# Word conversion of the first eight weight tiles and the first group's division in a fused attention, FFN and expert kernel

## The chip, the cores and the metric

One core of a Trainium2 chip runs the whole program. The metric is device time in microseconds (us) of one execution; the time before is the median of three runs.

## The reference, cut to what matters

Three stages follow one another over 4 x 576 = 2304 tokens of 512 channels (8 heads of 64).

```python
# 1 attention with random features, per batch and head
phi(x): proj = x @ omega.T; h = proj - |x|^2/2; exp(h - max(h)) / sqrt(m)      # m = 128
kv = k_p.T @ v ; z = sum(k_p) ; out = (q_p @ kv) / (q_p @ z + 1e-6)
# 2 feed-forward, w_in and w_out are float64
h = x @ w_in ; g = h * clip(h + 3, 0, 6) / 6 ; x = g @ w_out                    # 512 -> 2048 -> 512
# 3 top-1 of 8 experts
e = argmax(x @ w_gate + modality_bias[modality_id]) ; out = gate * (relu(x @ w1[e]) @ w2[e])
```

The weights `w_in` and `w_out` arrive as float64, so each value is two 32-bit words, and the kernel makes the float32 value of them on the chip.

## The kernel before, in words

The 2304 tokens are nine groups of 256 (`NG`), of two tiles of 128 rows (`GT`). The 8 heads are four pairs (`NPR`); a unit is one pair with one batch (for k) or with one group (for q).

*How the order is set.* No order is written out. Every piece of work is a generator that hands its next instruction to a list scheduler (`Issue.run`, line 255), which keeps a modelled clock for each engine (`cost`, line 79), takes the engine whose next instruction could start first, and among the instructions that could start within 0.08 us of that one the one with the lowest priority number. The program's instruction order on each engine is fixed by this when the program is built; on the chip each engine runs its list in order. Priorities: the first group's units -1.0 (`FIRST`), the feed-forward activations -0.8, the word conversions -0.3 (`CONVERT`), the weight splits -0.25, the loads -0.1, the products 0.05. An operation that may run on several engines is given to the one that the model says ends first.

*The first group.* `early(pr)`, line 1327, runs for each of the four pairs a k unit of batch 0 (`k_unit`) and then the q unit of group 0 (`q_unit`, line 804). Buffers for these come from the ring `w`, so the trace calls them all `w`. A q unit projects with TensorE, takes the maximum on VectorE (`mx`), takes four exponentials on ScalarE (`phi`, line 571), forms four sums with `z` on VectorE (`junk`, with the sum in `den`), adds a constant, takes the reciprocal, multiplies each of its four 128 x 128 blocks by its column of `den` (line 849, one instruction per block, on VectorE, ScalarE or GpSimd), transposes with TensorE (`ident`), copies to SBUF on ScalarE (`k.qe`), multiplies by `kv` on TensorE, and is copied as `x`. For group 0 the PSUM banks are kv/kp, y0/y1, qa/qb and h0/h1 for the four pairs.

*The words.* There are 32 tiles of float64 weights, tile j holding 128 x 512 word pairs: even j is a tile of `w_in`, odd j of `w_out` (`loads`, line 472). The first eight (`NW0`) land in the ring `w`, the others in four buffers `words`. `convert` (line 509) turns a tile into float32: ScalarE makes the three low bits from the upper 16 bits of the low words (an int32 out of uint16 values, line 519), VectorE ORs the sign in from the high word (line 523), ScalarE multiplies the high words by 2^-112 in place (line 526), and VectorE shifts them left by 3 and ORs them in (line 527). Three workers (`NC`) take tiles in turn, j, j+3, and so on; tiles from 8 on wait until the four first units are over.

*The feed-forward.* Step c of group 0 needs x of all four pairs and tile 2c (`t_in`, products into `h`), then `r` by ScalarE and VectorE, then tile 2c+1 (`t_out`, products into `y`). Group 0 multiplies the float32 tiles as they are; the groups after it use tiles split in two (`split_w`, line 543). While group 0's sixteen steps run, the k units of batches 1 to 3 (`kp`, `kv`) and the q units of group 1 (`qa`, `qb`) run between them.

Of the kernel before, what the change touches and what calls it, by code (L numbers as in the profile page):

```python
# [12 lines left out]
I32 = mybir.dt.int32  # L13
AF = mybir.ActivationFunctionType
ALU = mybir.AluOpType
# [19 lines left out]
def f32(ap):  # L35
    return ap.bitcast(F32)
# [9 lines left out]
class Issue:  # L46
# [178 lines left out]
    def op(self, e, m, cond=None, **kw):  # L225

        es = [e] if isinstance(e, str) else list(e)
        outs, ins = self.aps(kw)
        g = Gate([(x, ins, outs, self.cost(x, m, kw)) for x in es], cond)
        yield g  # L230
        x = es[g.pick]
        if x == "A" and m == "tensor_copy":
            kw = dict(out=kw["out"], in_=kw["in_"], func=AF.Copy)
            m = "activation"
        if x == "A" and m == "tensor_scalar":
            kw = dict(out=kw["out"], in_=kw["in0"], func=AF.Copy, scale=kw["scalar1"])
            m = "activation"
        self.do(x, m, **kw)
# [63 lines left out]
def favor_ffn_top1_moe_kernel(  # L302
# [37 lines left out]
    NW0 = 8  # L340
# [9 lines left out]
    do, op = q.do, q.op  # L350
# [47 lines left out]
    def split(hi, lo, src, hi_eng=("A", "V"), lo_eng="V"):  # L398
        yield from op(hi_eng, "tensor_copy", out=hi, in_=src)
        yield from op(lo_eng, "tensor_tensor", out=lo, in0=src, in1=f32(hi), op=ALU.subtract)  # L400

    def tt(o, a, b, f, e="V"):
        return op(e, "tensor_tensor", out=o, in0=a, in1=b, op=f)

    def ts(o, a, s1, f1, s2=None, f2=None, e="V"):
        kw = dict(out=o, in0=a, scalar1=s1, scalar2=s2, op0=f1)
        if f2 is not None:
            kw["op1"] = f2
        return op(e, "tensor_scalar", **kw)
# [54 lines left out]
    w_in_t, w_out_t, w_full = {}, {}, {}  # L464
# [3 lines left out]
    def conv():  # L468

        staged, whole, parts, done, cut, short, issued = {}, {}, {}, set(), set(), [], set()  # L470

        def loads():
            for j in range(NW):
                c = j // 2
                yield Gate(cond=lambda: st["early_k"] == n_streams and (j < NW0 + NB or j - NB in done))
                w = q.tile(*((wp, [P, DM, 2], I32, "w", NW) if j < NW0 else (const, [P, DM, 2], I32, "words", NB)))
                issued.add(j)
                if j % 2 == 0:
                    src = w_in[:, c * P:(c + 1) * P, :].rearrange("(k p) f w -> p k f w", p=P)
                    yield from op("S", "dma_start", out=w.rearrange("p (k f) w -> p k f w", k=KD), in_=src)  # L480
                else:
                    yield from op("S", "dma_start", out=w, in_=w_out[c * P:(c + 1) * P])
                staged[j] = w

            for j in range(NB):
                yield Gate(cond=lambda: NW - NB + j in done)
                w = q.tile(const, [P, E // NB, DM], F32, "words", NB)
                for e in range(E // NB):
                    yield from op("S", "dma_start", out=w[:, e], in_=w_gate[len(wg):len(wg) + 1, :].to_broadcast([P, DM]))
                    wg.append(w[:, e])  # L490

        def place(c, which):

            if c < WC:
                yield Gate(cond=lambda: c in whole)
                return whole[c][:, which, :]
            if len(short) >= 4 and short[-4] not in cut:
                yield Gate(cond=lambda: short[-4] in cut)
            short.append(2 * c + which)
            return q.tile(ff, [P, DM], F32, "st", 4)  # L500

        def places():
            yield Gate(cond=lambda: NW0 - 1 in issued)
            for c in range(WC):
                if c == NW - NW0 - 3 * n_streams:
                    yield Gate(cond=lambda: st["early"] == n_streams)
                whole[c] = q.tile(wp, [P, 2, DM], F32, "w", NW)

        def convert(j):
            c, which = j // 2, j % 2  # L510
            yield Gate(cond=lambda: j in staged)
            t = yield from place(c, which)
            w = staged.pop(j)
            lo_w, hi_w = w[:, :, 0], w[:, :, 1]


            ti = t.bitcast(I32)
            half = w.rearrange("p n w -> p (n w)").bitcast(U16).rearrange("p (n w) -> p n w", w=4)
            yield from op(
                "A", "activation", out=ti, in_=half[:, :, 1], func=AF.Copy, scale=2.0 ** -13, bias=2.0 ** -14 - 0.5  # L520
            )

            yield from op(
                "V", "scalar_tensor_tensor", out=ti, in0=hi_w, scalar=-(1 << 31), in1=ti, op0=ALU.bitwise_and, op1=ALU.bitwise_or
            )
            yield from ts(f32(hi_w), f32(hi_w), 2.0 ** -112, ALU.mult, e="A")
            yield from op(
                "V", "scalar_tensor_tensor", out=ti, in0=hi_w, scalar=3, in1=ti,
                op0=ALU.logical_shift_left, op1=ALU.bitwise_or,
            )  # L530
            done.add(j)
            w_full[which, c] = t

        def gone(k):

            if k < 3 * n_streams:
                return st["early"] == n_streams
            c = k - 3 * n_streams - NW0
            if c < 0:
                return c + NW0 in done  # L540
            return 2 * c in cut and 2 * c + 1 in cut and min(st["n_in"], st["n_out"]) > c

        def split_w(j):

            c, which = j // 2, j % 2
            yield Gate(cond=lambda: len(whole) == WC and (which, c) in w_full and len(parts) == j
                       and gone(j - NW + WC + NW0 + 3 * n_streams) and (c < WC or st["n_out" if which else "n_in"] > c))
            t = parts[j] = q.tile(wp, [P, 2, DM], F32R, "w", NW)
            yield from split(t[:, 0], t[:, 1], w_full[which, c], ("A", "P"))
            cut.add(j)  # L550
            (w_out_t if which else w_in_t)[c] = t

        def splitter(k, n):
            for j in range(k, NW, n):
                yield from split_w(j)

        def worker(k, n):
            for j in range(k, NW, n):
                if j >= NB * 2:
                    yield Gate(cond=lambda: st["early"] == n_streams)  # L560
                yield from convert(j)

        q.add(loads(), LOADS)
        q.add(places())
        for k in range(NC):
            q.add(worker(k, NC), CONVERT)
        for k in range(2):
            q.add(splitter(k, 2), CUT)
# [230 lines left out]
    def q_units(k, units, tag):  # L799
        for g, pr in units:  # L800
            yield from q_load(k, g, pr)
            yield from q_unit(k, g, pr, [tag])

    def q_unit(k, g, pr, tags):
# [10 lines left out]
        else:  # L815
# [7 lines left out]
            for t in range(GT):  # L823
                c = slice(t * P, (t + 1) * P)
# [11 lines left out]
        for t in range(GT):  # L836
            for o, n, b, s in runs(g * G + t * P, P):
                for h in range(2):
# [3 lines left out]
                        in1=z_t[b, pr][o:o + n, h, :], op0=ALU.mult, op1=ALU.mult, accum_out=den[o:o + n, i:i + 1],  # L842
                    )
        yield from ts(den, den, 1e-6 * M, ALU.add)
        yield from op("V", "reciprocal", out=den, in_=den)
        if k.two:
            yield from tt(qp, qp, den.unsqueeze(2).to_broadcast([P, 2 * GT, M]), ALU.mult)
        else:
            for i in range(2 * GT):
                yield from ts(qp[:, i], qp[:, i], den[:, i:i + 1], ALU.mult, e=("V", "A", "P"))  # L850
# [6 lines left out]
        for o, n, b, s in rr:  # L857

            for h in range(2):
                c = slice(h * D, (h + 1) * D)  # L860
# [447 lines left out]
    with ExitStack() as ph, tc.manual_schedule():  # L1308
# [18 lines left out]
        def early(pr):  # L1327
            k = k_bufs_early()
            yield from k_unit(k, 0, pr, early_banks[pr])
            yield Gate(cond=lambda: k.loaded > len(k_parts))  # L1330
            yield from q_unit(k, 0, pr, early_banks[pr][:2])
            st["early"] += 1
            gone_by.add(pr)
# [138 lines left out]
```

## Time and profile before

| | |
|---|---|
| time before, median of 3 runs | 834.08 us (831.96 to 835.83) |
| profiled execution, its own time | 834.48 us |
| its span in the trace | 832.8 us |
| TensorE busy over the span | 791.0 us (95%) |
| VectorE busy | 630.8 us (76%) |
| ScalarE busy | 487.1 us (58%) |
| GpSimd busy | 99.7 us (12%) |
| mean granted TensorE clock | 0.983 |

Busy shares are over the whole span; the stages differ much, so the views by stretch say more than this table. PE is TensorE, DVE VectorE, ACT ScalarE, POOL GpSimd, SP SyncE. All of the kernel's instructions are issued from one helper, so that every row carries line 223; the tiles tell them apart. The modelled end of a matmul includes time in which it waited in the pipeline.

### The profile page before, as it was taken

How to read it: one execution, taken by the hardware profiler on the slowest of the kernel's cores; microseconds unless marked ns; L12 is line 12 of the kernel's file. 1: busy time of each engine (PE TensorE's matmuls, PEld its weight loads, DVE VectorE, ACT ScalarE, POOL GpSimd, SP SyncE). 2: the span in 40 equal slices, each digit the busy share in tenths (PEclk: the TensorE clock that was granted, in tenths of full speed). 3: DMA queues.
4: the chain of work that ended last, by engine and by line, in shares of the span. 5: the costliest groups of instructions: out<-in, count | busy, mean ns of one | idle time of the engine just before them, and what ended most of it. 6: DMA issues, size and time to landing. Idle time of an engine off the chain costs nothing.

```text
span 832.8 us, 16519 instructions
## 1 busy us (share of the span) xinstructions
PE 791.0 (95%) x5395; PEld 675.0 (81%) x5395; DVE 630.8 (76%) x2135; ACT 487.1 (58%) x1245; POOL 99.7 (12%) x114
## 2 busy tenths in 40 slices
PE   7799999999999999999999999998995999999994
PEld 5476668888888888888888888987884898999993
DVE  3889999888888868878788785667986777777610
ACT  3998786777757556555655453335445766555411
POOL 0132342000000000110000000002013122211000
PEclk9989999999999999999999999999997999999997
DMA  7717574222113022221120010009359899877300
GB/s 182 278 52 228 168 243 132 51 54 83 51 33 81 13 53 68 32 61 47 41 64 27 1 39 1 26 15 289 94 171 293 276 289 273 270 219 207 103 13 29
DMA packets 108767, 96.88 MB, mean 116 GB/s; under 512 B 14847, under 2 KB 90111, under 8 KB 108672
## 3 DMA queue, kind: packets, MB, share of 16 engines
q1 hardware_dynamic: 104976, 85.75, 35.8%
q0 software_dynamic: 3696, 9.98, 3.5%
q8 instruction: 45, 0.74, 0.4%
q14 instruction: 50, 0.41, 0.2%
HBM read 86.10 MB, written 9.87 MB: 115 GB/s over the span
## 4 chain that ended last, share of the span: by engine, by line
issue 36%; PE 33%; DMA 15%; DVE 8%; ACT 4%; POOL 1%; SPq 1%; POOLq 0%; DVEq 0%; ACTq 0%
PE h L223 14%; PE y L223 9%; DMA wraw<-in_w_dram 5%; DMA order<-og,pi 4%; DVE w L223 4%; PE qa L223 3%; PE qb L223 3%; ACT w L223 2%; PE kv L223 2%; PE kp L223 2%; DMA xr<-yrows,src 1%; DMA kraw<-in_kT_dram 1%; SPq L223 1%; POOL order L223 1%; DMA w<-in_v_dram 1%
## 5 line engine op out<-in xcount | busy, mean ns | idle before, releaser
L223 PE MATMUL h<-x,w 128*128 128x256 f32 x2616 | 367.6, 290 | 2.1 <-DVE gl L223 0.9
L223 PEld LDWEIGHTS h<-x,w 128*128 128x128 f32 x2616 | 343.0, 191 | 22.5 <-issue 3.8
L223 PE MATMUL y<-w,gh 128*128 128x512 f32 x640 | 205.2, 402 | 0.0
L223 PE MATMUL y<-w,gl 128*128 128x512 f32 x320 | 126.0, 394 | 0.0
L223 PEld LDWEIGHTS y<-w,gh 128*128 128x128 f32 x640 | 110.2, 190 | 18.2 <-issue 3.0
L223 DVE TENSOR_TENSOR w<-wraw,w 128x512 fp32r<-128x512 f32 x160 | 106.3, 687 | 20.3 <-ACT w L223 16.4
L223 ACT ACTIVATE w<-wraw 128x512 fp32r<-128x512 f32 x152 | 91.2, 627 | 29.1 <-DMA wraw<-in_w_dram 25.7
L223 ACT ACTIVATE r<-h,three 128x256 f32<-128x256 f32 x144 | 68.1, 473 | 62.5 <-PE h L223 52.4
L223 DVE SCALAR_TENSOR_TENSOR junk<-st,words 128x512 bf16<-128x512 f32 x144 | 98.8, 686 | 1.2
L223 ACT ACTIVATE gh<-r 128x256 fp32r<-128x256 f32 x126 | 52.5, 417 | 80.3 <-PE y L223 75.1
L223 DVE SCALAR_TENSOR_TENSOR r<-r,h 128x256 f32<-128x256 f32 x144 | 60.3, 419 | 28.2 <-ACT r L223 24.8
L223 DVE TENSOR_TENSOR gl<-r,gh 128x256 fp32r<-128x256 f32 x128 | 54.3, 424 | 34.4 <-ACT gh L223 22.0
L223 PEld LDWEIGHTS y<-w,gl 128*128 128x128 f32 x320 | 60.5, 189 | 14.3 <-DVE gl L223 0.3
L223 POOL DMA_INDIRECT order<-og,pi x18 | 19.1, 1064 | 406.9 <-DVE pi L223 261.4
L223 ACT ACTIVATE gh<-h 128x256 fp32r<-128x256 f32 x72 | 27.4, 380 | 60.1 <-PE qb L223 22.4
L223 DVE SCALAR_TENSOR_TENSOR gl<-h,gh 128x256 fp32r<-128x256 f32 x72 | 30.4, 422 | 31.9 <-ACT gh L223 29.1
L223 ACT ACTIVATE kp<-kp,mx 112x128 f32<-112x128 f32 (+1 forms) x120 | 38.8, 387 | 1.2 <-DVE mx L223 1.0
L223 POOL DMA_INDIRECT out_dram<-st,tok x19 | 19.8, 1040 | 162.5 <-ACT gh L223 77.7
L223 DVE SCALAR_TENSOR_TENSOR junk<-qp,zb 128x128 bf16<-128x128 f32 (+1 forms) x144 | 37.4, 286 | 1.4 <-ACT qp L223 0.2
L223 ACT ACTIVATE qp<-qp,mx 128x128 f32<-128x128 f32 x104 | 36.2, 393 | 0.0
L223 DVE SCALAR_TENSOR_TENSOR w<-words,w 128x512 int32<-128x512 int32 x44 | 31.7, 748 | 0.0
L223 PE MATMUL kp<-om,khl 128*112 128x256 f32 (+1 forms) x140 | 29.4, 307 | 1.5 <-DVE khl L223 1.0
(270 smaller groups left out, 1069.4 us busy)
## 6 DMA issues: line engine op xcount, KB each, us to landing
wraw<-in_w_dram SPq DMA_DIRECT2D x160, 256.0 KB
words<-in_w_in_dram SPq DMA_DIRECT2D x12, 512.0 KB
words<-in_w_out_dram SPq DMA_DIRECT2D x12, 512.0 KB
qraw<-in_qT_dram SPq DMA_DIRECT2D x36, 128.0 KB
yrows<-st SPq DMA_DIRECT2D x18, 256.0 KB
kraw<-in_kT_dram SPq DMA_DIRECT2D x40, 112.0 KB
vraw<-in_v_dram SPq DMA_DIRECT2D x24, 112.0 KB
w<-in_w_in_dram SPq DMA_DIRECT2D x4, 512.0 KB
```

What stands on the lines that cost most here:

```text
L223: return getattr(self.eng[e], m)(**kw)
```

## The change

Two edits. In `convert`, the tiles with j below 8 take another way: ScalarE multiplies the high words by 2^-112 in place first; VectorE multiplies the result by 2^-126 into the output tile, which leaves only the sign; VectorE shifts the low words right by 29 and ORs the three bits in; VectorE shifts the high words left by 3 and ORs them in. The tiles from 8 on are as before. In `q_unit`, the units of group 0 multiply their four blocks by `den` with one VectorE instruction, as units with `k.two` did already.

```diff
@@ convert(j), after lo_w, hi_w = w[:, :, 0], w[:, :, 1]
+            if j < NW0:
+
+                ti = t.bitcast(I32)
+                yield from ts(f32(hi_w), f32(hi_w), 2.0 ** -112, ALU.mult, e="A")
+                yield from ts(t, f32(hi_w), 2.0 ** -126, ALU.mult)
+                for w_, n, f in ((lo_w, 29, ALU.logical_shift_right), (hi_w, 3, ALU.logical_shift_left)):
+                    yield from op(
+                        "V", "scalar_tensor_tensor", out=ti, in0=w_, scalar=n, in1=ti, op0=f, op1=ALU.bitwise_or
+                    )
+                done.add(j)
+                w_full[which, c] = t
+                return
@@ q_unit(k, g, pr, tags)
-        if k.two:
+        if k.two or not g:
             yield from tt(qp, qp, den.unsqueeze(2).to_broadcast([P, 2 * GT, M]), ALU.mult)
         else:
             for i in range(2 * GT):
                 yield from ts(qp[:, i], qp[:, i], den[:, i:i + 1], ALU.mult, e=("V", "A", "P"))
```

## Rows read from the trace of the kernel before

**Rows 1.** Busy time of each engine by stretch (count), granted clock, DMA share, GB/s.
```profile
20.00:30.00 10.00, 8.21 (x105) 5.70 (x104) 6.46 (x14) 7.95 (x30) 0.00 (x0) 1.00 1.00 363
30.00:40.00 10.00, 5.65 (x36) 4.14 (x36) 9.38 (x49) 9.84 (x33) 1.15 (x2) 0.96 0.65 228
40.00:50.00 10.00, 10.00 (x54) 6.67 (x54) 6.95 (x15) 9.07 (x25) 5.00 (x8) 0.70 0.18 49
60.00:80.00 20.00, 19.90 (x128) 14.11 (x128) 19.39 (x44) 17.36 (x46) 6.56 (x6) 1.00 0.76 238
100.00:150.00 50.00, 48.64 (x305) 36.06 (x303) 48.30 (x111) 39.43 (x98) 16.98 (x14) 1.00 0.53 162
600.00:700.00 100.00, 89.39 (x569) 80.32 (x568) 77.61 (x179) 59.64 (x124) 23.90 (x22) 0.95 0.86 258
```
**Rows 2.** Chain of waits from 18 to 60 us: start, length, what.
```profile
32.58 0.99 ACT w L223 x4
...
35.55 1.52 ACT w L223 x6
...
37.12 2.64 ACT w L223 x6
...
39.80 1.12 PE kv L223 x4
40.92 1.35 PE y L223 x4
...
47.38 1.73 PE h L223 x8
```
**Rows 3.** ScalarE's groups by form, 28 to 46.7 us: busy, mean ns, idle before.
```profile
L223 ACT ACTIVATE w<-w 128x512 f32<-128x512 f32 x6 | 4.3, 776 | 0.0
L223 ACT ACTIVATE w<-w 128x128 f32<-128x128 f32 x10 | 3.3, 436 | 0.0
L223 ACT ACTIVATE w<-w 128x512 int32<-128x512 uint16 x4 | 2.7, 717 | 0.0
```
**Rows 4.** ScalarE in order of time: start, length, instruction, count.
```profile
38.01 0.69 ACT L223 ACTIVATE w<-w 128x512 int32<-128x512 uint16 x1
38.58 0.68 ACT L223 ACTIVATE w<-w 128x512 int32<-128x512 uint16 x1
41.88 0.72 ACT L223 ACTIVATE w<-w 128x128 f32<-128x128 f32 x2
42.17 0.43 ACT L223 ACTIVATE w<-w 128x128 f32<-128x128 f32 x1
```
**Rows 5.** VectorE in order of time, in brackets its idle time before.
```profile
27.53 0.42 DVE L223 TENSOR_REDUCE mx<-qb 128x2 f32<-128x256 f32 x1 [1.56 <-PE qb L223]
31.63 1.28 DVE L223 SCALAR_TENSOR_TENSOR w<-w 128x512 int32<-128x512 int32 x2
43.69 0.84 DVE L223 SCALAR_TENSOR_TENSOR w<-w 128x512 int32<-128x512 int32 x1 [0.81 <-ACT w L223]
46.20 0.69 DVE L223 SCALAR_TENSOR_TENSOR w<-w 128x512 int32<-128x512 int32 x1 [1.68 <-ACT w L223]
```
**Rows 6.** Groups by form of the whole run: busy, mean ns, idle before.
```profile
L223 DVE TENSOR_TENSOR qp<-qp,den 128x512 f32<-128x512 f32 x26 | 17.9, 687 | 0.2
L223 DVE SCALAR_TENSOR_TENSOR w<-w 128x512 int32<-128x512 int32 x16 | 11.1, 705 | 2.6 <-ACT w L223 2.5
L223 DVE CAST w<-wraw 128x512 fp32r<-128x512 f32 x8 | 3.4, 426 | 1.6 <-DMA wraw<-in_w_dram 1.6
```
**Rows 7.** The first group's blocks on GpSimd, 20 to 60 us, by form.
```profile
L223 POOL TENSOR_SCALAR w<-w 128x128 f32<-128x128 f32 x5 | 4.0, 806 | 36.1 <-DVE junk L223 36.1
```
**Rows 8.** TensorE by microsecond: stretch, busy, granted clock, DMA share, GB/s.
```profile
36.00:37.00 1.00, 0.00 (x0) 1.00 0.19 62
...
39.00:40.00 1.00, 0.20 (x2) 0.57 0.00 0
40.00:41.00 1.00, 1.00 (x5) 0.50 0.00 0
...
46.00:47.00 1.00, 1.00 (x11) 1.00 0.00 0
```

## The prediction

> **What bounds the kernel now.** I read the busy time by stretch first, then the chain of waits through the stretch that the change touches, then the engines' own order there, and last the groups by form for prices.
>
> The stretches [rows 1] show two regimes. From 60 us on TensorE is the bound: 19.90 of 20 us, 48.64 of 50. From 20 to 40 us it is not: 8.21 and 5.65 of 10, while ScalarE is busy for 7.95 and then 9.84, and VectorE for 6.46 and then 9.38. Everything that the diff touches lies in this start, before the first product of the feed-forward at 47.4 us. What the change can bring is therefore the time at which that first product starts; behind it TensorE has the same products to do, and I carry the shift to the end one for one.
>
> The chain of waits [rows 2] says what that start hangs on. Its rows from 32.58 through 39.76 us are ScalarE's, nearly without a break (16 exponentials, three divided blocks, word conversions, a copy): about 7.2 us in which the chain follows ScalarE. Then TensorE takes over at 39.80, and the chain stays on it until the first product. TensorE's own microseconds [rows 8] show why those take so long: it did nothing from 36 to 37, and from 39 to 46 us the granted clock is about 0.5, the lower of its two levels (1.2 GHz), with the engine busy all the time from 40 on. It rises again in the microsecond from 46.
>
> So there are three parts: ScalarE up to 39.8, TensorE at its lower level up to 46, TensorE at 2.4 GHz after it. VectorE is nearly as full as ScalarE from 30 to 40 us, and that is what decides this case.
>
> **The change part by part.** *Prices.* ScalarE's word instructions start 0.57 us apart (38.01, 38.58) and its divided blocks 0.29 apart (41.88, 42.17) [rows 4]. Of VectorE's word instructions two in a row take 1.28 us, so 0.6 us each from start to start, beside a duration of 0.705 [rows 5, 6]. The new division is an operation that later units already use: 128 x 512 by `den` takes 0.687 us [rows 6], again 0.6 from start to start.
>
> *The multiplication by 2^-126* has no row: 128 x 512 float32, one input that skips every other word. From below, the nearest is the cast of a dense 128 x 512 tile, 0.426; from above, the two-input word instruction on the same skipping input, 0.705 [rows 6]. It reads a single tensor in SBUF like the first and skips like the second. I take the middle, 0.55, and keep both ends: 3.4 to 5.6 us for eight of them. The Trainium skill, VectorE: DVE Perf Modes, section "What auto-detection actually checks", asks for a single source and a destination in SBUF with fitting outer dimensions for its two-results mode and names no dense step; by that rule the price is the lower end, and the eight cost 3.4 us instead of my 4.4. No row of this trace shows that mode on a skipping input.
>
> *What ScalarE loses.* One instruction of each of the eight tiles, 8 x 0.57 = 4.6 us, and ten divided blocks, 10 x 0.29 = 2.9 us [rows 3, 4]: 7.5 in all. From 28 to 46.7 us it had 6 + 4 word instructions [rows 3]; six tiles would now need six. Of the chain's 7.2 us on ScalarE, two conversions (1.14) and three blocks (0.88) go: 2.0 us, and one more conversion at most, 2.6. But a tile that follows sooner puts its own ScalarE instruction into the freed place, because the three workers no longer pass to and fro between the engines (before: ScalarE, VectorE, ScalarE, VectorE; now ScalarE once, then VectorE three times). I take half of 2.6: a gain of 1.3 us.
>
> *What VectorE gains.* Eight multiplications, 4.4, and four divisions of 0.6, 2.4, less a block that it did itself: about 6.6 us, where it stood still for 1.56, 0.81 and 1.68 us at the three largest breaks between 25 and 47 us [rows 5], 4.05 together. The words have slack: the first product needs tile 0, its second stage tile 1, and a step takes two tiles, so the later of the eight can be done after 47 us. What has no slack is the four sums of each unit before the reciprocal. The first unit's division (0.6) now stands ahead of other units' sums on VectorE: a loss of 0.6. The other three divisions follow their own sums and replace ScalarE's and GpSimd's blocks (five, 4.0 us of GpSimd [rows 7]), which were spread over three engines; TensorE at its lower level takes some 1 us for a unit's four transposes, longer than the 0.6 of a division, so these are hidden behind the unit before. If TensorE ran at 2.4 GHz that cover would be gone, at 0.1 us a unit or so.
>
> *What stays.* From 40.92 us TensorE itself sets the pace, and neither edit removes anything there. The conversions' order of loads and the queue of SyncE get nothing new; a buffer of tiles 0 to 7 comes free at most about 0.6 us later.
>
> *Sum.* -1.3 + 0.6 = -0.7 us at the first product. The profiled execution took 834.48 us, 1.7 more than its span of 832.8 and 0.4 more than the median; on the median the sum is 834.08 - 0.7 = 833.4 us. About 0.5% (4.2 us) is what a measurement of this kernel tells from no change.
>
> **The rivals.** *Faster: ScalarE was the whole bound.* The chain lies on ScalarE for 7.2 us, which speaks for it. Then all of the 2.6 us goes, and with TensorE resuming earlier its clock may not fall: the stretch from 40.9 to 46 at the lower level, 5.1 us, would take half, 2.6 less. Together 834.1 - 5.2 = 828.9 us. Against it: VectorE at 9.38 of 10 from 30 to 40 us [rows 1] has no room to follow, and the idle microsecond from 36 to 37 [rows 8] waits on the sums of VectorE as well.
>
> *Slower: VectorE becomes the bound of the start.* Place: the sums from 34 to 40 us. Each word instruction that VectorE begins just before a maximum or a sum is ready holds it for up to 0.6 us, and now up to three of a tile stand ready at once. If six of the eight multiplications at the upper price (0.6 from start to start, 3.6) and the first three divisions (1.8) lie ahead of the last sum, the first product comes 5.4 us later, less 0.6 that ScalarE gives: 838.9 us. It decides from the point at which more than 4.8 us of the added work lies ahead of that sum. Against it: the priority of the first units (-1.0 against -0.3) lets a word in only where nothing of theirs is ready.
>
> *Another order later.* The scheduler's modelled clocks move, so the order of all instructions behind may differ. From 600 to 700 us TensorE stands still for 10.6 us [rows 1], in the stage where transfers of expert weights arrive; such gaps can grow or shrink by a few us whatever the start does. Priced at 3 to 5 us of either sign: 829 or 838 us. Against it: the products and their transfers are the same, and in the stretches from 60 to 150 us little is idle that could change.
>
> *No effect at all*, because the freed ScalarE time and the added VectorE time cancel: 834.1, which is inside the forecast's own case.
>
> **How the numbers follow.** Forecast (0.58): the shift lies between -3 and +3 us, 831 to 837, likeliest 833.4. ScalarE the whole bound: 0.17. VectorE the bound: 0.10. Another order: 0.15, of which 0.08 faster by over 0.5%, 0.04 slower and 0.03 within. Faster 0.25, within 0.5% 0.61, slower 0.14. The range from 828 to 838.5 takes in the faster rival's value and nearly the slower one's; some 0.15 lies outside it.
>
> **What would show it.** In the profile of the changed kernel: ScalarE's busy time from 20 to 50 us falls by 4 to 7 us and VectorE's rises by about as much, with its breaks gone; the multiplication by 2^-126 takes between 0.43 and 0.70 us; the first product of the feed-forward starts at 46.7, give or take 2; TensorE's lower level appears around 39 to 46 us again. The forecast is wrong if the first product moves by over 4 us, if TensorE's clock holds through 40 to 46 us, or if the first product stands where I say and the end moves otherwise: then it was the order of the later stages.

## The result: 1.4% slower, and little of it in the start

| | before | after |
|---|---|---|
| median on the same chip | 834.96 us (831.96 to 836.29, 4 runs) | 846.10 us (839.29 to 850.46, 4 runs) |
| ratio, 95% interval | | 1.0137 (1.0102 to 1.0172) |
| profiled execution, its span | 834.48, 832.8 us | 842.66, 840.6 us |
| TensorE busy over the span | 791.0 us | 791.8 us |

The change loses 11.1 us by the medians; the two profiled executions lie 8.2 apart, and all readings of the traces below are about those 8.2. TensorE's busy time hardly moved, so nearly all of the loss is time in which TensorE stood still: 832.8 - 791.0 = 41.8 us before, 840.6 - 791.8 = 48.8 after.

First, stretches of after, which answer to [rows 1] (same columns):

```profile
20.00:30.00 10.00, 7.28 (x68) 4.76 (x64) 7.82 (x17) 7.32 (x22) 0.91 (x2) 0.74 1.02 365
30.00:40.00 10.00, 6.88 (x57) 5.40 (x56) 8.52 (x32) 8.47 (x33) 0.44 (x1) 0.92 0.79 259
40.00:50.00 10.00, 7.81 (x43) 4.92 (x44) 9.77 (x36) 5.99 (x16) 0.00 (x0) 0.83 0.04 11
100.00:150.00 50.00, 47.25 (x322) 35.80 (x321) 47.26 (x107) 37.11 (x97) 13.69 (x15) 1.00 0.47 150
600.00:700.00 100.00, 86.88 (x543) 76.06 (x542) 78.51 (x184) 63.35 (x132) 21.41 (x19) 0.93 0.83 248
```

In the start the engines did what the edits ask: from 20 to 50 us ScalarE is busy for 21.78 us against 26.86, and VectorE for 26.10 against 22.79. But TensorE also lost in 100 to 150 and in 600 to 700 us, where neither edit has an instruction. The prices of the edits, VectorE from 20 to 60 us by form (answers to [rows 6]) and all that GpSimd does there (to [rows 7]):

```profile
L223 DVE SCALAR_TENSOR_TENSOR w<-w 128x512 int32<-128x512 int32 x16 | 10.5, 684 | 0.1
...
L223 DVE TENSOR_SCALAR w<-w 128x512 f32<-128x512 f32 x8 | 3.4, 429 | 0.0
...
L223 DVE TENSOR_TENSOR w<-w 128x512 f32<-128x512 f32 x4 | 2.7, 686 | 0.0
```
```profile
L223 POOL CAST w<-w 128x512 fp32r<-128x512 f32 x2 | 1.4, 676 | 26.3 <-DVE w L223 26.3
L223 POOL TENSOR_SCALAR qp<-qp,den 128x128 f32<-128x128 f32 x1 | 0.6, 614 | 28.1 <-DVE den L223 28.1
```

The eight multiplications by 2^-126 took 0.429 us each, the four divisions 0.686; GpSimd's five blocks are gone. TensorE around the first product, by microsecond (to [rows 8]) and in order of time (start, length, what, in brackets the idle time before and what ended it):

```profile
40.00:41.00 1.00, 0.00 (x0) 1.00 0.00 0
41.00:42.00 1.00, 0.34 (x2) 0.89 0.00 0
42.00:43.00 1.00, 0.96 (x5) 0.50 0.00 0
```
```profile
41.66 1.05 PE L223 MATMUL kp<-ident,w 128*128 128x128 f32 x4 [4.79 <-DVE w L223]
...
49.03 1.99 PE L223 MATMUL h<-x,w 128*128 128x256 f32 x8 [0.48 <-ACT x L223]
```

The first product of before, in the same view:

```profile
47.22 1.89 PE L223 MATMUL h<-x,w 128*128 128x256 f32 x8
```

In after TensorE waits 4.79 us for VectorE's `w`, resumes at 41.66 us (before it does the same product at 37.61 us, after a wait of 3.07, and waits once more up to 39.80, [rows 2]), works at the lower level (granted clock 0.50) and starts the first product at 49.03 us, 1.8 later than the same product of before (47.22 us; the 47.38 of [rows 2] counts from the end of the work ahead of it). Between these two traces that is a little over a fifth of the 8.2.

The start varies from one execution to another, though, and the traces say by how much. Four traces hold the program of before up to the first product (before, and three kernels below that change only what comes later: its two nudges and the routing put first): the product starts at 47.22, 48.23, 47.85 and 47.95 us. Four hold that of after (after, its two nudges, "new then old"): 49.03, 48.20, 50.49 and 51.76 us. The granted clock from 20 to 30 us was 1.00 in the trace of 48.20 (the row below, TensorE alone) and 0.74 to 0.89 in the other three. So the changed start came later in most traces, but the 1.8 us are one draw out of a wide spread.

```profile
20.00:30.00 10.00, 7.34 (x102) 1.00 1.01 367
```

Where is the rest of the 8.2? TensorE's busy time over the whole run, cut where the kernel's stages change (stretch, busy, granted clock, DMA share, GB/s), first before, then after:

```profile
16.00:47.00 31.00, 24.87 (x212) 0.89 0.68 233
47.00:150.00 103.00, 101.17 (x627) 1.00 0.53 164
150.00:300.00 150.00, 150.00 (x1141) 1.00 0.21 55
300.00:545.00 245.00, 243.03 (x1698) 1.00 0.14 36
545.00:700.00 155.00, 141.32 (x887) 0.96 0.71 213
```
```profile
16.00:47.00 31.00, 23.45 (x189) 0.83 0.68 228
47.00:150.00 103.00, 99.19 (x627) 1.00 0.50 160
150.00:300.00 150.00, 147.65 (x1131) 1.00 0.21 53
300.00:545.00 245.00, 243.53 (x1704) 1.00 0.14 38
545.00:700.00 155.00, 138.92 (x859) 0.94 0.68 203
```

Subtract line by line: 1.42 us lost up to 47, 1.98 up to 150, 2.35 up to 300, 0.50 won back, 2.40 lost from 545 to 700. Behind 47 us that makes 6.2 us net (1.98 + 2.35 - 0.50 + 2.40), where but for the last word tiles the code is the same in both kernels. What differs there is the order of the instructions on each engine. Three waits of TensorE in after, one from each losing stretch, and under them the like of the last one in before:

```profile
118.08 1.78 PE L223 MATMUL h<-x,w 128*128 128x256 f32 x7 [1.56 <-DVE w L223]
...
268.25 0.48 PE L223 MATMUL qa<-om,qhl 128*128 128x256 f32 x2 [1.74 <-DVE qhl L223]
...
639.32 0.45 PE L223 MATMUL kp<-ident,xr 128*128 128x128 f32 x1 [9.04 <-DMA xr<-yrows,src]
```
```profile
632.50 0.45 PE L223 MATMUL kp<-ident,xr 128*128 128x128 f32 x1 [7.97 <-DMA xr<-yrows,src]
```

They are of different kinds: a weight tile on VectorE, a q unit's input split, the gather of rows for the experts. The longest wait of before from 100 to 150 us was 0.6 us, from 150 to 300 TensorE was busy for all 150.00; only the last has its like there (7.97 us). The waits name no single culprit.

### The profile page after: what moved, and what is told of

It is laid out like the page before. It is cut to its first block, busy times and chain, and to the rows that moved or that the text cites. A ratio compares the mean times of both kernels' runs of the same rounds, so it can differ in the third digit from the quotient of the medians.

```text
span 840.6 us, 16421 instructions
## 1 busy us (share of the span) xinstructions
PE 791.8 (94%) x5399; PEld 673.8 (80%) x5399; DVE 630.0 (75%) x2118; ACT 489.8 (58%) x1239; POOL 94.9 (11%) x113
## 5 line engine op out<-in xcount | busy, mean ns | idle before, releaser
L223 DVE TENSOR_TENSOR w<-wraw,w 128x512 fp32r<-128x512 f32 x160 | 108.5, 690 | 30.5 <-ACT w L223 27.3
L223 ACT ACTIVATE w<-wraw 128x512 fp32r<-128x512 f32 x159 | 97.7, 629 | 42.2 <-DMA wraw<-in_w_dram 32.7
L223 ACT ACTIVATE qp<-qp,mx 128x128 f32<-128x128 f32 x96 | 34.0, 393 | 0.0
```

What stands on the lines that cost most here:

```text
L223: return getattr(self.eng[e], m)(**kw)
```

## The experiments

Two theories. *The work*: the added VectorE work delays the start and what follows it. *The order*: `Issue.run` chooses by its modelled clocks, so changing a few instructions early draws another order for all that comes later, and that order is worse on the chip. Each pair of medians below is from one chip; "before" is its median there. The steps in the tables are 16 of group 0 (0 to 15), 16 for each later group (16 to 143) and then the experts (from 144); a step's time is the start of its first product into `h`, found in each trace by counting the products.

### One edit alone

```diff
 words_alone: the changed kernel, with
-        if k.two or not g:
+        if k.two:
 division_alone: the kernel before, with
-        if k.two:
+        if k.two or not g:
```

> Only the first edit (the words of tiles 0 to 7), the division as before. The start theory (VectorE's added instructions delay the first product of the feed-forward, and the delay is carried to the end): eight more VectorE instructions of 0.35 us from start to start, about 2.8 us, so the first product at 48 to 50 us (47.2 before) and the time 1 to 3 us above before, 835 to 837. The order theory (the moved modelled clocks redraw the order of all later instructions, and the stage of the experts from 545 to 700 us pays): the first product within 1.5 us of before, the time anywhere from 830 to 848, with the loss after 545 us.

> Only the second edit (one VectorE instruction divides a unit of group 0), the words as before. The start theory: four divisions of 0.6 us on VectorE against ten blocks taken from ScalarE, so within 1 us of before either way, 833 to 835. The order theory: again a redraw, the time anywhere from 830 to 848, and it need not add up with the other edit to the whole change.

Measured, with before at 833.81 us: words alone 840.40 us (835.34 to 842.63), 1.0093 (1.0070 to 1.0115); division alone 847.88 us (845.33 to 852.27), 1.0178 (1.0149 to 1.0206). The parts don't add up: the division costs more alone (14.1 us) than both edits do together (11.1). For both edits the start theory's time is missed and the order theory's range holds. Whether the words' loss comes after 545 us, as the order theory had it, can't be read: their only trace is of the fastest execution (835.34 us, 5 us under the median). In the trace of division alone the first product starts at 47.35 us, 0.13 after before's; 7.6 us are lost between there and step 24, in waits such as this one:

```profile
134.94 0.46 PE L223 MATMUL kp<-om,khl 128*112 128x256 f32 x2 [2.61 <-DVE khl L223]
```

This speaks against *the work*: sixteen blocks made into four instructions, all done before 47 us, leave nothing behind that could hold a later batch's k units at 135 us when the first product was on time. It doesn't yet show that the order did.

### The work and the order crossed

The order of before was written down as the sequence in which the scheduler picked its tasks and their engines (4768 picks, of which 4756 are left for the changed work), and the scheduler made to follow that list. The work is untouched by this; only who goes next.

```diff
 Issue.run
-                s, e = min(x[:2] for x in found)
-                _, _, t, k = min((x for x in found if x[1] == e and x[0] <= s + self.eps), key=...)
+                s, k = ORDER[self.pos]
+                t = ready.get(s)
+                self.pos += 1
```

`new_work_old_order` has both edits and the sequence of before, less the picks that the edits take away. `old_work_new_order` has the words and the division of before in the sequence of the changed kernel; a unit's four blocks go one behind another where the one division stood.

> Both edits, but the scheduler is made to take every piece of work in the sequence in which it was taken in the kernel before (recorded there and forced here), so that behind the start each engine's list is the same as before. The order theory: the whole loss goes, 832 to 836 us, and the stage from 545 to 700 us takes what it took before. The start theory: the loss of the start stays and with it that of the end, 840 us or more.

> The words and the division as in the kernel before, but every piece of work is taken in the sequence of the changed kernel (the four blocks of a division one after the other where the one instruction stood). The order theory: the loss appears without the edits' instructions, 840 to 850 us, with a wide spread between runs. The start theory: about 834 us, as before.

| median, ratio to 833.81 us | old order | order of the changed kernel |
|---|---|---|
| old work | 833.81 us | 843.53 us, 1.0127 (1.0107 to 1.0147) |
| changed work | 834.61 us, 1.0010 (0.9994 to 1.0025) | 846.10 us, 1.0137 on its own chip |

The order alone costs 9.7 us, the work alone 0.8 us, with an interval that holds zero. Both times lie where the order theory had them, neither where the start theory had them. TensorE by stretch, changed work in the old order, then old work in the changed order:

```profile
16.00:47.00 31.00, 23.46 (x207) 0.89 0.69 232
47.00:150.00 103.00, 101.39 (x627) 1.00 0.53 164
150.00:300.00 150.00, 150.00 (x1141) 1.00 0.21 55
```
```profile
47.00:150.00 103.00, 98.51 (x625) 1.00 0.50 160
150.00:300.00 150.00, 147.87 (x1123) 1.00 0.21 53
...
545.00:700.00 155.00, 138.51 (x860) 0.96 0.67 203
```

With the old order the stretch from 150 to 300 us has no gap again; with the new one the old work shows the losses of after, stretch for stretch. The lateness of steps against before, in us, follows the order and not the work:

| step (before starts at) | after | changed work, old order | old work, changed order | division alone | nudged by 0.2 |
|---|---|---|---|---|---|
| 0 (47.22) | +1.81 | +0.48 | +2.68 | +0.13 | +1.01 |
| 24 (153.28) | +1.84 | +0.14 | +2.55 | +7.69 | +2.21 |
| 80 (357.80) | +7.54 | -0.61 | +8.03 | +12.72 | +3.63 |
| 96 (422.30) | +0.44 | -0.54 | +0.86 | +13.16 | +13.27 |
| 143 (565.47) | +2.36 | -1.00 | +2.79 | +11.54 | +13.46 |
| 168 (659.62) | +8.56 | -3.16 | +9.64 | +13.37 | +14.58 |
| 216 (801.23) | +9.12 | -2.74 | +9.04 | +15.46 | +15.50 |

(The fall from +7.5 to +0.4 at step 96 is other work, k and q units, done at another time; a step's lateness is not idle time. Each column is one trace. "New then old", below, has the program of after up to step 128 and is 3.78 us late at step 96 where after is 0.44, so a difference of about 3 us between two columns can be that of two executions.)

The crossed kernel also answers what the work does to the start when the order is held. Its chain of waits there (start, length, what), to be set beside [rows 2], and VectorE's own order of time under it:

```profile
31.84 1.80 DVE w L223 x3
...
38.00 0.60 DVE w L223
38.60 1.27 DVE junk L223 x12
...
41.11 0.68 DVE w L223 x2
41.83 1.12 PE y L223 x4
```
```profile
30.56 0.68 DVE L223 SCALAR_TENSOR_TENSOR w<-w 128x512 int32<-128x512 int32 x1
...
31.76 1.89 DVE L223 SCALAR_TENSOR_TENSOR w<-w 128x512 int32<-128x512 int32 x3
...
36.20 0.51 DVE L223 TENSOR_SCALAR w<-w 128x512 f32<-128x512 f32 x2
...
37.91 0.69 DVE L223 TENSOR_TENSOR w<-w 128x512 f32<-128x512 f32 x1
...
40.08 0.69 DVE L223 SCALAR_TENSOR_TENSOR w<-w 128x512 int32<-128x512 int32 x1
...
41.11 0.67 DVE L223 TENSOR_TENSOR w<-w 128x512 f32<-128x512 f32 x1
```

The chain that lay on ScalarE from 32.58 to 39.76 us now lies nearly all on VectorE, up to 41.8. The tile `w` hides several things, which the order of time tells apart: word instructions at 30.56, 31.76 and 40.08, a multiplication of the words at 36.20 (with a small addition behind it in the row), the first unit's division at 37.91, ahead of the sums (`junk`) of another unit, and a second division at 41.11. TensorE's wait for the first unit's blocks says the same. Before, then the changed work in the old order, and the latter's first product:

```profile
37.61 0.91 PE L223 MATMUL kp<-ident,w 128*128 128x128 f32 x4 [3.07 <-ACT w L223]
```
```profile
38.66 0.66 PE L223 MATMUL kp<-ident,w 128*128 128x128 f32 x4 [4.12 <-DVE w L223]
...
47.70 1.89 PE L223 MATMUL h<-x,w 128*128 128x256 f32 x8
```

The wait of about 3.07 us for ScalarE stands in all four traces with the start of before, that of 4.12 us for VectorE in both traces with the changed work in the old order there (the second is "old then new", below). So VectorE did become the bound of the start. What it cost at the first product is too little to tell: the product starts at 47.70 and 47.52 us in these two traces, inside the 47.22 to 48.23 us of the four.

### Where in the order the loss lies

```diff
 new_order_then_old: both edits; picks of the changed kernel up to step 128, then those of before
 old_order_then_new: both edits; picks of before up to step 128, then those of the changed kernel
```

> Both edits. The work is taken in the changed kernel's sequence up to the first product of the ninth group (step 128, at 525 us in the changed kernel's trace), and what is left in the sequence of the kernel before. If the loss sits in the order of the last routing and of the expert stage: 835 to 838 us, the 2.4 us that step 128 was late and no more. If it sits in the order of the first 525 us and is only seen later: 843 us or more.

> The other way round: both edits, the sequence of the kernel before up to step 128, and the changed kernel's sequence behind it. If the loss sits in the order of the last routing and of the expert stage: 839 to 843 us, with step 144 and step 168 late by 3 and 6 us more than step 128. If it sits in the first 525 us: 833 to 836.

Measured, with before at 833.67 us: new then old 839.27 us, 1.0074 (1.0048 to 1.0101); old then new 837.11 us, 1.0045 (1.0029 to 1.0061). Both times lie between the two that had been expected of each. Behind step 128 a pick that isn't ready is passed over until it is, so the second half follows the named sequence nearly, not exactly. The excesses, 5.6 us (4.0 to 8.4) and 3.4 us (2.4 to 5.1), sum to 9.0, near the 9.7 of the whole order. So there is no one place: by the medians some six tenths lie before step 128 and four tenths behind it. Of the second part one link can be read. GpSimd's writes of the routing for groups 7 and 8 (the last in the feed-forward), before and then after:

```profile
550.76 0.97 POOL L223 DMA_INDIRECT order<-og,pi  x1 [31.78 <-DVE pi L223]
...
611.05 0.97 POOL L223 DMA_INDIRECT order<-og,pi  x1 [0.30 <-DVE w L223]
```
```profile
555.94 0.97 POOL L223 DMA_INDIRECT order<-og,pi  x1 [33.12 <-DVE pi L223]
...
619.01 1.43 POOL L223 DMA_INDIRECT order<-og,pi  x1 [0.30 <-DVE w L223]
```

They start 5.2 and 8.0 us later, where the products of step 143 are 2.4 late; TensorE's first use of the rows gathered for the experts behind the second write is 6.8 late (632.50 before, 639.32 after). TensorE stood waiting for that gather in both kernels, 7.97 us before and 9.04 after, so there is nothing in between that would hide a later write.

### Another order with the same work

If any redrawing of the order costs this much, before must get slower with no edit at all. One line adds a constant to the scheduler's modelled clock of VectorE, once, at the first product; no work is added, taken away or changed (which of several allowed engines does an operation can change with the order).

```diff
 t_in, behind step_in(x) of step i
+                if i == 0:
+                    q.clk["V"] += 0.2        # nudge_large: 1.2
```

> The kernel before with no edit of its work; at the first product of the feed-forward 0.2 us is added to the scheduler's modelled clock of VectorE, so that the program up to there is the same and all behind it is ordered anew. If the kernel before is one draw among orders of unequal worth, and the change only draws another: a time that differs from 834 by more than 4 us is likely, 836 to 848. If what costs is something that the edits themselves bring into the order: 832 to 836.

> The same with 1.2 us. If an order drawn anew is worth anything from 830 to 850: again a time off 834 by several us, and not in proportion to the nudge. If not: 832 to 836.

> The changed kernel with both edits; at the first product of the feed-forward 0.2 us is added to the scheduler's modelled clock of VectorE, so that all behind it is ordered anew. If the loss is the worth of the one order that the change happened to draw: another time, anywhere from 833 to 850 us. If the new work draws bad orders by its nature: 842 to 850, near the changed kernel.

> The same with 1.2 us. If each order is a draw: anywhere from 833 to 850 us, and not in proportion to the nudge. If the new work draws bad orders by its nature: 842 to 850.

Measured: before nudged by 0.2 us 847.35 (847.25 to 848.51), 1.0171 (1.0150 to 1.0193); by 1.2 us 839.67, 1.0076 (1.0047 to 1.0106), before at 833.67. The changed kernel nudged by 0.2 us 839.87, 1.0067 (1.0041 to 1.0092); by 1.2 us 840.42, 1.0072 (1.0045 to 1.0099), before at 833.06. So the same work in another draw costs up to 13.7 us, the smaller nudge of before costs more than the larger, and the changed kernel got *better* by both nudges, below the 842 us that would have spoken for bad orders by nature. Yet none of its three draws comes near before (11.1, 6.8 and 7.4 us above it); those of the old work cost 13.7 and 6.0. Before nudged by 0.2 loses its time at another place than after, between steps 80 and 96, where one of TensorE's waits is for a q unit's input split:

```profile
429.56 0.80 PE L223 MATMUL qa<-om,qhl 128*128 128x256 f32 x2 [2.31 <-DVE qhl L223]
```

### One aimed repair

The link through the routing suggested putting it first: its priority in the kernel before raised far above the rest.

```diff
-ROUTE = 0.05, -0.05
+ROUTE = 0.05, -0.9
```

> The kernel before with one priority changed: the routing of the last two groups and the tables of the experts go ahead of the feed-forward's activations (-0.9 in place of -0.05), so that the program up to the end of the eighth group is the same. If TensorE's longest stand in the expert stage (10.3 us near 632 us in the kernel before) waits on the routing's place in VectorE's list: the last writes of the routing come 5 us or more earlier against step 143 and that stand shrinks by as much, while TensorE waits up to 8 us more for activations near 525 and 580 us; 830 to 838 in all. If the stand waits on the transfers alone: it stays at 9 to 11 us and the time is 836 to 845.

Measured: 838.99 us (836.41 to 839.97), 1.0059 (1.0039 to 1.0080). TensorE's waits in it:

```profile
541.02 2.29 PE L223 MATMUL h<-x,w 128*128 128x256 f32 x9 [7.42 <-DVE r L223]
...
599.87 1.44 PE L223 MATMUL h<-x,w 128*128 128x256 f32 x5 [8.30 <-DVE gl L223]
...
636.01 0.55 PE L223 MATMUL kp<-ident,xr 128*128 128x128 f32 x3 [2.60 <-DMA xr<-yrows,src]
```

The long wait for the gather shrank from 7.97 to 2.60 us, as meant (the 10.3 us of the expectation is all of TensorE's idle time from 620 to 665 us in before, not one stand), but two new ones of 7.42 and 8.30 us stand ahead of it: VectorE did the routing while the activations of the feed-forward (`r`) and then of the experts (`gl`) waited. The time is 1 us above the 838 expected with a shorter wait. This priority moved the stall; no kernel tried beats before.

## Why the prediction was wrong

**The step that failed** is the sentence "behind it TensorE has the same products to do, and I carry the shift to the end one for one". The products are the same (busy 791.0 and 791.8 us); their order is not, and TensorE's idle time grew by 7.0 us. The rival "Another order later" named the mechanism but was mis-sized in three ways. Its price was 3 to 5 us; the eight orders other than before's that the scheduler drew by itself (after, each edit alone, four nudges, the routing) cost 5.9 to 14.1. Its sign was taken as even or better; all eight were slower. Its chance was 0.15; it decided the case. The argument against it, that "in the stretches from 60 to 150 us little is idle that could change", read a full TensorE as safe. It is the reverse: 48.64 of 50 and, further on, 150.00 of 150 busy means that a redrawn order could hardly win there, only lose. Nor does everything that the diff touches lie ahead of the first product, as the prediction has it: in before, four of the sixteen word instructions of these tiles on VectorE begin behind it, at 48.03 to 55.53 us; the prediction itself gives the later tiles slack, so nothing hung on this.

**The start, -0.7 us forecast.** Held to the old order, the shift can't be told from zero (47.70 and 47.52 us against 47.22 to 48.23), which is inside the forecast's own -3 to +3 and shows neither the gain nor a loss. In the order that the change drew, the first product of after stands at 49.03 us, just past the forecast's 46.7 give or take 2. ScalarE's fall (5.1 us, forecast 4 to 7) was right. VectorE's rise was 3.3, less than the "about as much", and its breaks shrank but stayed: the three largest from 25 to 47 us in after are 1.07, 0.79 and 0.59 us, 2.45 together where before had 4.05. The multiplication was mis-sized: 0.429 us, not 0.55. The Trainium skill, VectorE: DVE Perf Modes, section "What auto-detection actually checks", would have given that lower end, and the trace agrees on an input that skips every other word (0.429 us, against 0.426 for the dense cast of [rows 6]). The 1.3 us of gain on ScalarE's side isn't seen, although the eight multiplications were 1 us cheaper than forecast: TensorE's wait for the first unit's blocks became longer (3.07 us for ScalarE, 4.12 for VectorE). That freed ScalarE time brings nothing once VectorE's maxima, sums and words set the start is argued from this chain; no run freed ScalarE without giving VectorE more. The 0.6 for the first unit's division ahead of other units' sums was right (0.60 us on the chain, at 38.00).

**VectorE becomes the bound** was right in kind (the chain above) and not in size, a shift that can't be told from zero instead of 4.8 us: the word instructions on that chain are some 3.3 us (0.6 from start to start each: one at 30.56, three at 31.76, one at 40.08; about 0.3 for the multiplication at 36.20) and two divisions 1.2 more, and they take the place of ScalarE's 7.2 us on it. **ScalarE the whole bound** fell: TensorE's clock went to the lower level again (0.50 from 42 us on). **No effect at all** is what the work did; the kernel's time was decided elsewhere.

**What is still open.** Why the order of before is better than every other drawn; the kernel has priorities and penalties set by hand, and no run here tells whether they were set by trying orders. Of the part of the loss before step 128 some waits are named, but which pick starts it wasn't tried. Nor is it known why one and the same start takes 48.20 us in one execution and 51.76 in another.

## What to carry to other kernels

Where a list scheduler writes the order, an edit is two changes, its instructions and a new draw of everything behind it; separate them by forcing the old sequence on the new work and the new sequence on the old work. To know the size of a draw before predicting, give the model a small meaningless nudge and time that: here the work was worth 0.1%, with an interval that holds zero, and a draw 0.6 to 1.8%. Take several traces of one program before you call a difference of 1 or 2 us at one product a cost. When the bound engine is already busy 97 to 100% of a stretch, expect a new draw to lose there.

## What was not expected of the hardware

The four runs of one and the same changed program spread over 11.2 us (839.29 to 850.46), those of before on that chip over 4.3 (831.96 to 836.29). It is tempting to call the order less steady, but the record doesn't show that: the same order with the old work spreads over 3.4 us in six runs (841.95 to 845.30), though a wide spread was expected, and before nudged by 0.2 us, slower still, over 1.3 in five. Some of the spread arises in the start, which differs by 3.6 us among four traces of the same instructions; where the rest arises stays open. A single profile can lie several us from its program's median, as that of after does (842.66 against 846.10) and that of words alone (835.34 against 840.40).
